# Attention and gated MLP on one core: stores off ScalarE, reciprocals on GpSimd's queue, diagonal copies on ScalarE

## The chip, the cores and the metric

The kernel runs on 1 core of one Trainium2 chip. The metric is device time in microseconds (us) of one execution. A core has five engines with instruction queues of their own: PE (TensorE, matmuls), ACT (ScalarE), DVE (VectorE), POOL (GpSimd) and SP (SyncE, which only issues transfers). Each works through its queue in order; an instruction whose inputs are not there holds up everything behind it. Transfers are issued from SP, ACT or POOL and carried out by 16 DMA engines.

## What is computed

Causal attention in blocks of 64 (8 batches, 8 heads, 576 rows, head size 64), then a gated MLP on its output. In short:

```python
scores = scale * q @ k.T                      # masked by blocks of 64
attn = exp(scores - max) / (sum + 1e-9)
x = (attn @ v)  -> [4608, 512]
gate = 1 / (1 + exp(-(x @ w_gate)))           # w_gate, w_val: 512 x 1536
out = (gate * (x @ w_val)) @ w_out            # w_out: 1536 x 512
```

Precision is kept by splitting each float32 operand into a high and a low part and by three matmuls for each product.

## The kernel before

**Stages.** A *pair* is two heads of one batch; there are 32 pairs (`pairs`), four for each batch. Pairs 0 to 7 follow an order written out by hand (`FRONT`); while that runs, `scripted` is not empty. Pairs 8 to 31 run in the loop at lines 1208 to 1249, and beside their attention the matmuls of the first MLP (the first 512 of the 1536 hidden columns, `mlp1`, `mlp_out`) are dealt out between PE's steps, 36 for each pair. From about 610 us the second MLP (lines 1429 to 1465) does the other 1024 columns and adds the partial results.

**One pair p in the loop**, in the order of `REST`: scores and exponentials (`s`, `t`); then AV of the pair before (`av`, 22 float32 matmuls, which the trace counts as 44; here called AV(p-1)) and its scaling by the reciprocals (`xT`, line 675); block transposes of the exponentials on DVE (`turn`, line 589); preparation of the next pair's keys and queries (`prep`: pm, kl and qx are POOL's part, lines 395, 398 and 408); `move`; `finish` of pair p-1; `recip` of pair p; loads of the keys and queries of pair p+3 (8 transfers) and of the values of pair p+2 (3).

**move (line 591)** is there for pairs 8 to 30 (`moved`). The exponentials lie in `Z` (for odd pairs in the memory of `XB`, which is how the profile then names it) and are rearranged into `G` by 12 transfers of 32 partitions by 800 float32 each, 6 issued on SP and 6 on POOL, and by four copies of the diagonal blocks, 2 on ACT (line 603) and 2 on POOL (line 600). `G` is one buffer: moves of pair p can only start when AV(p-1) has read it, and AV(p) needs them landed.

**recip (line 554).** DVE forms reciprocals of the row sums and transposes them into `rT` (128 x 32). Four transfers on SP store rows 0 to 8 of each of its four 32-row blocks into a DRAM tile `r_d`; three transfers on SP read that back, broadcast over 64 partitions each, into `rb`. `issue` (line 291) keeps transfers on SP behind the last of SP's moves.

**finish (line 799)** of pair p-1: ACT rounds `xT` into `XH` (kept behind the last diagonal copy on ACT), ACT issues the store of `xT` to `xT_d` (288 KB), POOL forms the low part `XL` (kept behind the last of POOL's moves). `out_store` (line 912): ACT halves an MLP result into `ost` and issues its store to `part_d` (256 KB); some one for each pair.

**Order.** Beyond such fixed orders (`behind`) the order of each engine's queue comes from a planner at compile time, which simulates the program and takes what it believes to be ready. On the chip that order is fixed.

Of the kernel before, what the change touches and what calls it, by code (L numbers as in the profile page):

```python
# [9 lines left out]
F32 = mybir.dt.float32  # L10
# [63 lines left out]
def attn_glu_kernel(ctx: ExitStack, tc: tile.TileContext, q, k, v, w_gate, w_val, w_out, out):  # L74
    nc = tc.nc
    B, H, S, D = q.shape
    NTOK, DM = out.shape
    DF = w_gate.shape[1]
    P = 128
# [6 lines left out]
    dram = ctx.enter_context(tc.tile_pool(name="dram", bufs=1, space=DRAM))  # L86
    xT_d = dram.tile([B, DM, S], F32, name="xT_d")
    part_d = dram.tile([NTOK, DM], F32, name="part_d")
# [12 lines left out]
    def behind(ins, other):  # L101

        tc.add_manual_dep(ins, other.name, mybir.DependencyInfo(mybir.DependencyClass.NoSync,
                                                                mybir.DependencyReason.DATA), reason="order")

    def engine_of(queue):

        return "SP" if queue is nc.sync else "ACT" if queue is nc.scalar else "POOL"
# [119 lines left out]
    with ExitStack() as s2:  # L228
# [14 lines left out]
        def x_tiles(b):  # L243

            i = b % 2
            if i not in X:
                X[i] = [(xp0 if i else xp1).tile([P, NC, S], F32R, name=f"X{e}{i}") for e in "HL"]
            return X[i]
# [20 lines left out]
        pairs = [(b, hp) for b in range(B) for hp in range(NP)]  # L269
# [21 lines left out]
        def issue(queue, **kw):  # L291
            ins = queue.dma_start(**kw)  # L292
            if queue is nc.sync and "moves" in last:
                behind(ins.ins, last["moves"])
            return pin(engine_of(queue), ins, True)

        def load(p, what, queue=nc.sync, part=None):
# [33 lines left out]
        last = {}  # L331
        maxima, exps = [], []

        scripted = {}

        def mark(engine, ins):
            last[engine] = ins.ins

        def pin(engine, ins, dma=False):

            if scripted.get("on"):
                for turn in (engine, "DMA") if dma else (engine,):
                    if turn in scripted:
                        behind(ins.ins, scripted[turn])
                    scripted[turn] = ins.ins
                mark(engine, ins)
            return ins
# [24 lines left out]
        def rows(h):  # L372
            return slice(64 * h, 64 * h + 64)
# [47 lines left out]
        def attend(p):  # L421
            b, hp = pairs[p]
            KQ, QB, VS = state.pop(p)
            sm = SMs[p % 2]
            keep = {}
# [12 lines left out]
            Zc = Zs[p % 2].rearrange("p (c x) -> p c x", c=4)  # L438
            Gc = Gt[:, :4 * WB].rearrange("p (a x) -> p a x", a=4)

            def xT_():
                return tile_of("xT", [S])
# [4 lines left out]
            def rb_():  # L447
                return tile_of("rb", [S])
# [3 lines left out]
            moved = N_FIRST < p < len(pairs) - 1  # L452
# [43 lines left out]
            def s_blocks(*groups):  # L496

                maxima.clear()
                exps.clear()
                tiles = [two_banks() for _ in groups]  # L500
                for k, (ps, group) in enumerate(zip(tiles, groups)):
                    for j, i in enumerate(group):
                        scores(ps, i, 2 * P * j)
                        if rest and dealt and k == j == 0:
                            behind(first_mm[0], dealt[-1])
                if rest:
                    hold[:] = pe_last
                for ps, group in zip(tiles, groups):
                    n = P * (group[0] + 1)
                    if len(group) == 1:  # L510
                        nc.vector.memset(ps[0:64, :, n - 64:n], -1e9)
                    else:
                        nc.vector.memset(ps[0:64, :, P:3 * P].rearrange("p h (i n) -> p h i n", i=2)[:, :, :, 64:], -1e9)
                    for j, i in enumerate(group):
                        softmax(ps, i, 2 * P * j)
# [38 lines left out]
            def recip(part=None, queue=nc.sync):  # L554


                if part in (None, 0):
                    pin("DVE", nc.vector.tensor_scalar_add(sm[:, :9], sm[:, :9], 1e-9))
                    pin("DVE", nc.vector.reciprocal(sm[:, :9], sm[:, :9]))
                    keep["rT"] = at.tile([P, 32], F32, name="rT", bufs=2)  # L560
                    mark("DVE", pin("DVE", nc.vector.transpose(out=keep["rT"], in_=sm)))
                if part in (None, 1):
                    keep["r_d"] = dram.tile([9, P], F32, name="r_d", bufs=2)
                    for j in range(4):
                        issue(queue, out=keep["r_d"][:, 32 * j:32 * j + 32], in_=keep["rT"][32 * j:32 * j + 9])
                if part in (None, 2):
                    r_f = keep["r_d"].rearrange("c q -> (c q)")
                    for h, o, n, f in ((0, 0, S, 0), (1, 4 * P, D, S), (1, 0, 4 * P, S + D)):
                        issue(queue, out=rb_()[rows(h), o:o + n], in_=r_f[f:f + n].partition_broadcast(D))

# [15 lines left out]
            def turn(lo, hi):  # L586

                z = Zc[:, :, 32 * lo:32 * hi]
                mark("DVE", nc.vector.transpose(out=z, in_=z))  # L589

            def move():

                turn(LT, NB)
                for k, (c, a) in enumerate(itertools.permutations(range(4), 2)):
                    ins = (nc.sync if k % 2 else nc.gpsimd).dma_start(out=Gc[32 * c:32 * c + 32, a], in_=Zc[32 * a:32 * a + 32, c])  # L595
                    mark("moves" if k % 2 else "POOL", ins)
                for c in range(4):
                    q = slice(32 * c, 32 * c + 32)
                    if c % 2:
                        ins = nc.gpsimd.tensor_copy(out=Gc[q, c], in_=Zc[q, c])  # L600
                        behind(ins.ins, last["POOL"])
                    else:
                        mark("ACT", nc.scalar.copy(out=Gc[q, c], in_=Zc[q, c]))

            def tr_main(i):
                if moved:
# [192 lines left out]
            def finish():  # L799
                XH, XL = x_tiles(b)  # L800
                cut = nc.scalar.copy(out=XH[:, hp], in_=xT_())
                if p == len(pairs) - 1:
                    mark("ACT", cut)
                nc.scalar.dma_start(
                    out=xT_d[b, hp * P:(hp + 1) * P, :], in_=xT_())
                low = nc.gpsimd.tensor_sub(out=XL[:, hp], in0=xT_(), in1=XH[:, hp].bitcast(F32))
                if "POOL" in last and p < len(pairs) - 2:
                    behind(low.ins, last["POOL"])
                    behind(cut.ins, last["ACT"])

            def step(what, is_fine=False, alt=False, queue=nc.sync):
                if is_fine:
                    fine(what, alt, queue)
                elif what == "s":
                    s_blocks((3,), (2,), (1, 0))
                elif what[0] == "s":
                    s_blocks({"s3": (3,), "s2": (2,), "sl": (1, 0)}[what])
                elif what == "t":
                    s_tail()
                elif what == "r":  # L820
                    recip()
                elif what == "trm":
                    if moved:
                        move()
                elif what in ("tr3", "tr2"):
                    tr_main(int(what[2]))
                elif what == "trl":
                    tr_low()
                elif what == "trt":
                    tr_tail()  # L830
                elif what == "fin":
                    finish()
                else:
                    av()
# [77 lines left out]
        def out_store(b, t, po):  # L912
            ost = mp.tile([P, DM], F32, name="t" if b == B and t > 1 else "ost", bufs=2)
            pin("ACT", nc.scalar.mul(out=ost, in_=po, mul=0.5))  # L914

            def store():
                if b < B:
                    r = b * S + t * P
                    pin("ACT", nc.scalar.dma_start(out=part_d[r:r + P, :], in_=ost), True)
                else:  # L920
                    for j in range(2):
                        r = (2 * t + j) * S + NM
                        nc.gpsimd.dma_start(out=part_d[r:r + 64, :], in_=ost[64 * j:64 * j + 64, :])

            return store
# [229 lines left out]
        for item in FRONT.split():  # L1155
            what, where = item.split(".")
            alt = where[-1] == "@"
            queue = nc.scalar if alt else nc.gpsimd if where[-1] == "#" else nc.sync
# [7 lines left out]
            p = int(where)  # L1166
# [41 lines left out]
        for p in range(N_FIRST + 1, n + 1):  # L1208
# [4 lines left out]
            for what, places in REST:  # L1213
# [17 lines left out]
                for _ in range(places if now else 6 if what == "AV" else 0):  # L1231
                    pe_ticks.append(pe_last[0])
                    acc += rate
                    while acc >= 1:
                        acc -= 1
                        left -= 1
                        ins = next(mlp, None)
# [257 lines left out]
```

## Time and profile before

| | us |
|---|---|
| median of 3 runs | 1166.02 |
| the runs | 1158.78 to 1166.15 |
| the profiled execution | 1164.24 |
| its span, first to last instruction | 1162.4 |
| outside the span | 1.8 |
| busy in the span: PE, DVE, ACT, POOL | 1106.7, 850.7, 582.0, 478.8 |

The stretch in which pairs 8 to 30 are worked on runs from about 127 to 505 us. A view of stretches gives the busy time of each engine in it, the granted TensorE clock as a share of 2.4 GHz (0.50 would be the lower level, 1.2 GHz) and the share of time that the 16 DMA engines were busy. In a timeline a row is a start, a duration and the work; `x6` joins six instructions; in brackets stands how long the engine sat idle before it, and what it is believed to have waited for. SPq and ACTq are transfers being issued; their duration is the time that the issuing queue spent.

### The profile page before, as it was taken

What the parts mean: (1) busy time and instruction counts of PE and PEld (TensorE: products, weight loads), DVE (VectorE), ACT (ScalarE), POOL (GpSimd) and SP (SyncE); (2) the same over time, 40 slices, a digit from 0 to 9 for tenths busy, and PEclk for the clock granted to TensorE, in tenths of its full rate; (3) what the DMA queues carried; (4) which work ended last, traced back from release to release, by engine and by line L of the source; (5) the groups of instructions that cost most, each with busy time, mean ns of one, the idle gap of its engine ahead of it and who ended that gap; (6) DMA issues with size and microseconds to landing.
All of it is one profiled execution on the core that took longest, in us unless ns stands there. A gap on an engine that the chain in (4) does not pass through costs nothing.

```text
span 1162.4 us, 19555 instructions
## 1 busy us (share of the span) xinstructions
PE 1106.7 (95%) x6593; PEld 946.8 (81%) x6593; DVE 850.7 (73%) x1482; ACT 582.0 (50%) x1298; POOL 478.8 (41%) x606
## 2 busy tenths in 40 slices
PE   8999989989989998879999999999999999999998
PEld 6677667777767776657889999899999998998998
DVE  7999886777757777738859977876876756756754
ACT  6887665656646665633335444444453332422421
POOL 3655475675656577522002303123033253262350
PEclk9999999999989999979999999999999999999999
DMA  8787577877787788753403335415298445263451
GB/s 171 171 182 167 128 173 187 205 158 192 174 191 158 190 185 164 182 153 107 152 30 109 101 113 208 136 73 208 81 334 281 158 139 171 69 196 116 120 164 55
DMA packets 270692, 181.64 MB, mean 156 GB/s; under 512 B 204576, under 2 KB 225312, under 8 KB 269952
## 3 DMA queue, kind: packets, MB, share of 16 engines
q1 hardware_dynamic: 248080, 143.90, 46.5%
q10 hardware_dynamic: 17712, 21.30, 5.7%
q0 software_dynamic: 4800, 15.19, 5.2%
q8 instruction: 52, 0.85, 0.3%
q14 instruction: 48, 0.39, 0.1%
HBM read 104.73 MB, written 47.33 MB: 131 GB/s over the span
## 4 chain that ended last, share of the span: by engine, by line
PE 70%; DMA 12%; DVE 6%; SPq 5%; issue 3%; ACT 2%; POOL 2%; ACTq 0%; DVEq 0%; POOLq 0%
PE b L1268 30%; PE m L1338 11%; PE bank L351 8%; PE m L179 6%; PE b L1338 6%; PE m L188 4%; SPq L292 3%; DMA G<-XB 3%; PE bank L179 3%; DMA G<-Z 2%; DMA r_d<-rT 1%; DMA XB<-xT_d 1%; DVE Z L589 1%; SPq L595 1%; PE bank L188 1%
## 5 line engine op out<-in xcount | busy, mean ns | idle before, releaser
L1268 PE MATMUL b<-XH,w 128*128 128x384 f32 x1344 | 349.1, 335 | 0.3 <-ACT t L914 0.3
L1268 PEld LDWEIGHTS b<-XH,w 128*128 128x128 f32 x1344 | 243.8, 188 | 4.3 <-ACT t L914 0.7
L1268 PE MATMUL b<-XL,w 128*128 128x384 f32 x672 | 223.5, 335 | 0.0
L351 PE MATMUL bank<-G,VS 128*64 128x64 f32 (+3 forms) x1264 | 110.0, 335 | 27.7 <-DMA r_d<-rT 17.5
L1268 PEld LDWEIGHTS b<-XL,w 128*128 128x128 f32 x672 | 126.1, 188 | 1.7
L351 PEld LDWEIGHTS bank<-G,VS 128*64 128x64 f32 x1264 | 77.8, 154 | 59.6 <-issue 23.8
L1084 POOL TENSOR_TENSOR XB<-XB 128x384 f32<-128x384 f32 x20 | 22.4, 1119 | 238.9 <-DMA XB<-xT_d 169.9
L1338 PE MATMUL m<-wo,hH 128*128 128x512 f32 x368 | 119.9, 391 | 0.0
L188 PE MATMUL m<-wo,hH 128*128 128x512 f32 x256 | 90.0, 403 | 2.7 <-ACT ost L914 2.7
L179 PE MATMUL m<-XH,wg 128*128 128x512 f32 x240 | 86.8, 409 | 0.0
L480 DVE TENSOR_REDUCE nm<-bank 128x2 f32<-128x1024 f32 (+1 forms) x96 | 77.1, 803 | 11.7 <-ACT Z L492 6.0
L1291 ACT ACTIVATE g<-g 128x384 f32<-128x384 f32 x72 | 37.9, 526 | 93.6 <-DVE g L1304 50.6
L179 PE MATMUL m<-XH,wv 128*128 128x512 f32 x240 | 84.4, 401 | 0.0
L1097 ACT CAST XH<-XB 128x1536 fp32r<-128x1536 f32 (+2 forms) x72 | 65.2, 941 | 37.0 <-DVE XB L1095 28.2
L1338 PEld LDWEIGHTS m<-wo,hH 128*128 128x128 f32 x368 | 69.0, 188 | 12.9
L1098 DVE TENSOR_TENSOR XL<-XB,XH 128x1536 fp32r<-128x1536 f32 (+2 forms) x72 | 75.8, 1085 | 0.0
L492 ACT ACTIVATE Z<-bank,nm 128x512 f32<-128x512 f32 (+3 forms) x104 | 53.7, 534 | 37.2 <-DMA G<-XB 16.2
L1338 PE MATMUL m<-wo,hL 128*128 128x512 f32 x184 | 72.1, 392 | 0.0
L1338 PE MATMUL b<-wo,hH 128*128 128x512 f32 (+1 forms) x216 | 71.4, 383 | 0.0
L492 ACT ACTIVATE XB<-bank,nm 128x512 f32<-128x512 f32 (+3 forms) x88 | 45.5, 530 | 37.1 <-DMA G<-Z 19.0
L188 PEld LDWEIGHTS m<-wo,hH 128*128 128x128 f32 x256 | 48.2, 189 | 15.6 <-ACT ost L914 3.5
L1332 POOL TENSOR_TENSOR pr<-pr,pr 128x512 f32<-128x512 f32 x33 | 42.9, 1307 | 41.2 <-DMA pr<-part_d 33.0
(217 smaller groups left out, 2537.5 us busy)
## 6 DMA issues: line engine op xcount, KB each, us to landing
pr<-part_d SPq DMA_DIRECT2D x66, 256.0 KB
xT_d<-xT ACTq DMA_DIRECT2D x32, 288.0 KB
XB<-xT_d SPq DMA_DIRECT2D x16, 576.0 KB
part_d<-pr SPq DMA_DIRECT2D x36, 256.0 KB
rqk<-in_q_dram SPq DMA_DIRECT2D x120, 72.0 KB
rqk<-in_k_dram SPq DMA_DIRECT2D x120, 72.0 KB
out_dram<-pr SPq DMA_DIRECT2D x33, 256.0 KB
part_d<-ost ACTq DMA_DIRECT2D x32, 256.0 KB
```

What stands on the lines that cost most here:

```text
L179: mm = nc.tensor.matmul(ps, lhsT=lh, rhs=rh, start=(i == 0), stop=(i == n - 1))
L188: mm = nc.tensor.matmul(ps, lhsT=lh[:, f, t * P:(t + 1) * P], rhs=rh, start=(f == i == 0), stop=(f == F1 - 1 and i == 2))
L292: ins = queue.dma_start(**kw)
L351: pe_last[:] = [pin("PE", nc.tensor.matmul(*args, **kw)).ins]
L480: mark("DVE", nc.vector.tensor_reduce(out=nm_()[:, c0:c0 + 2], in_=ps[:, :, c:c + n], axis=AX.X, op=ALU.max, negate=True))
L492: mark("ACT", nc.scalar.activation(out=dst, in_=src, func=AF.Exp, bias=nm_()[:, c0 + h:c0 + h + 1], accum_out=sm[:, 5 * h + i:5 * h + i + 1]))
L1097: nc.scalar.copy(out=XO[j][0][:, a:b], in_=x)
L1098: sub = nc.vector.tensor_sub(out=XO[j][1][:, a:b], in0=x, in1=XO[j][0][:, a:b].bitcast(F32))
L1268: mm = nc.tensor.matmul(ps, lhsT=lh, rhs=rh, start=(first and k == 0), stop=(k == n - 1), skip_group_check=not first)
L1291: mark2("ACT", nc.scalar.activation(out=t, in_=c, func=AF.Tanh, scale=0.5))
L1332: nc.gpsimd.tensor_add(out=pr[t], in0=pr[t], in1=other)
L1338: mm = nc.tensor.matmul(po[t][:, cols], lhsT=lh[:, f, t * P:(t + 1) * P], rhs=wo[:, f, e, cols], start=((whole or half == 0) and i == 0), ...
```

## The change

Six edits, all in effect for pairs 8 to 30 and the MLP beside them:

1. `recip` of a moved pair issues on POOL instead of SP. One transfer stores all of `rT` (128 partitions by 128 bytes, `r_d` now 32 rows) instead of four that store 9 rows each.
2. `issue` keeps a transfer on POOL behind `last["POOL"]`: the store of `rT` behind POOL's last move of the pair, and the three broadcasts behind the subtraction `XL` of pair p-1 (`last["low"]`).
3. All four diagonal copies are on ACT, none on POOL.
4. The store of `xT` is issued on SP for all pairs that `finish` handles but the last.
5. The store of `ost` is issued on SP, but for the part under `FRONT` and the last batch.
6. ACT therefore issues no transfer beside pairs 8 to 30.

```diff
         def issue(queue, **kw):
             ins = queue.dma_start(**kw)
             if queue is nc.sync and "moves" in last:
                 behind(ins.ins, last["moves"])
+            if queue is nc.gpsimd and "POOL" in last:
+                behind(ins.ins, last["POOL"])
...
-                    keep["r_d"] = dram.tile([9, P], F32, name="r_d", bufs=2)
-                    for j in range(4):
+                    keep["r_d"] = dram.tile([32, P], F32, name="r_d", bufs=2)[:32 if moved else 9]
+                    if moved:
+                        issue(queue, out=keep["r_d"].rearrange("c (j q) -> j c q", q=32), in_=keep["rT"])
+                    for j in range(0 if moved else 4):
...
+                    if moved:
+                        last["POOL"] = last["low"]
...
-                    if c % 2:
-                        ins = nc.gpsimd.tensor_copy(out=Gc[q, c], in_=Zc[q, c])
-                        behind(ins.ins, last["POOL"])
-                    else:
-                        mark("ACT", nc.scalar.copy(out=Gc[q, c], in_=Zc[q, c]))
+                    mark("ACT", nc.scalar.copy(out=Gc[q, c], in_=Zc[q, c]))
...
-                nc.scalar.dma_start(
+                (nc.sync if p < len(pairs) - 1 else nc.scalar).dma_start(
                     out=xT_d[b, hp * P:(hp + 1) * P, :], in_=xT_())
...
+                    last["low"] = low.ins
...
-                    recip()
+                    recip(None, nc.gpsimd if moved else nc.sync)
...
-                    pin("ACT", nc.scalar.dma_start(out=part_d[r:r + P, :], in_=ost), True)
+                    if scripted or b >= B - 1:
+                        pin("ACT", nc.scalar.dma_start(out=part_d[r:r + P, :], in_=ost), True)
+                    else:
+                        nc.sync.dma_start(out=part_d[r:r + P, :], in_=ost)
```

## Rows read from the trace of the kernel before

**Rows 1.** Busy us by stretch; columns: engines, PEclk, DMA share, GB/s.

```profile
146.50:478.80 332.30, 300.44 (x2143) 236.46 (x2143) 242.99 (x420) 203.29 (x521) 211.27 (x320) 0.95 0.80 180
610.00:1163.00 553.00, 549.26 (x2892) 513.54 (x2892) 390.86 (x666) 216.01 (x377) 166.28 (x151) 1.00 0.44 149
```

**Rows 2.** The same view of two single pairs and of 4 us.

```profile
379.10:393.80 14.70, 14.70 (x111) 11.65 (x112) 12.08 (x21) 9.50 (x25) 9.91 (x15) 1.00 0.72 158
393.80:410.10 16.30, 14.89 (x112) 11.54 (x112) 11.44 (x20) 10.27 (x26) 8.78 (x15) 1.00 0.87 212
...
218.00:222.00 4.00, 2.33 (x38) 2.06 (x40) 4.00 (x6) 3.02 (x9) 2.92 (x3) 1.00 0.36 79
```

**Rows 3.** The chain that ended last, 196 to 262 us, shares by line.

```profile
by line: SPq L292 18.8%; DMA G<-XB 14.1%; PE bank L351 13.0%; PE m L179 9.6%; DMA G<-Z 9.6%; SPq L595 9.1%; DMA xT_d<-xT 7.1%; DMA r_d<-rT 7.0%; DMA rqk<-in_q_dram 5.6%; PE m L188 3.4%; issue 3.0%; DVE Z L589 2.8%; DVE XB L589 1.7%; DVE h L
```

**Rows 4.** SP's timeline: first moves, one whole pair, last moves.

```profile
129.14 4.31 SPq L595 DMA_DIRECT2D G<-Z  x6
...
210.79 5.76 SPq L595 DMA_DIRECT2D G<-XB  x6
216.65 1.55 SPq L292 DMA_DIRECT2D r_d<-rT  x4
218.47 0.87 SPq L292 DMA_DIRECT2D rqk<-in_k_dram  x2
219.53 1.76 SPq L292 DMA_DIRECT2D rb<-r_d  x3
221.33 1.13 SPq L292 DMA_DIRECT2D rqk<-in_k_dram  x2
222.50 2.91 SPq L292 DMA_DIRECT2D rqk<-in_q_dram  x4
225.45 1.98 SPq L292 DMA_DIRECT2D VS<-in_v_dram  x3
227.54 5.17 SPq L595 DMA_DIRECT2D G<-Z  x6
...
493.88 8.23 SPq L595 DMA_DIRECT2D G<-Z  x6
```

**Rows 5.** All engines' timeline, 218 to 236 us: AV, POOL, scaling, AV.

```profile
219.67 2.97 PE L351 MATMUL bank<-G,VS 128*64 128x256 f32 x44 [2.64 <-DMA r_d<-rT]
...
223.53 3.02 POOL L595 DMA_DIRECT2D G<-Z  x6 [0.20 <-issue]
...
224.09 0.82 DVE L675 TENSOR_TENSOR xT<-bank,rb 128x320 f32<-128x320 f32 x2 [1.02 <-DMA rb<-r_d]
...
228.72 1.42 POOL L806 TENSOR_TENSOR XL<-xT,XH 128x576 fp32r<-128x576 f32 x1
...
235.23 0.98 PE L351 MATMUL bank<-G,VS 128*64 128x256 f32 x10 [1.14 <-DMA r_d<-rT]
```

**Rows 6.** ACT's timeline round one store of `ost`.

```profile
327.31 0.60 ACT L914 ACTIVATE ost<-m 128x512 f32<-128x512 f32 x1 [3.03 <-PE m L188]
331.77 0.33 ACTq L919 DMA_DIRECT2D part_d<-ost  x1
332.65 0.69 ACT L492 ACTIVATE XB<-bank,nm 128x512 f32<-128x512 f32 x1 [4.75 <-DMA G<-Z]
```

**Rows 7.** Waits, 127 to 505 us: total us, times, longest.

```profile
ACT XB L492 <- DMA G<-Z: 19.0, 6, 4.8
ACT Z L492 <- DMA G<-XB: 16.2, 6, 3.9
```

**Rows 8.** Single lines: ns min/median/max of one; last, us to landing of L595 on POOL.

```profile
L923 POOL DMA_DIRECT2D part_d<-ost x4: 521/523/554, 609.3 to 610.9; - x4
L600 POOL COPY G<-Z x24: 842/848/852, 133.8 to 496.0; 32x800 f32<-32x800 f32 x24
L603 ACT COPY G<-Z x24: 856/859/865, 129.2 to 491.8; 32x800 f32<-32x800 f32 x24
...
DMA to landing us min/median/max: 2.5/4.6/8.5
```

## The prediction

> **What bounds the kernel now.** The first view to read is that of stretches [rows 1]. From 610 us on PE is busy 549.26 of 553.00 us at full clock: nothing that the change touches is there. From 146.50 to 478.80 us, inside the stretch of pairs 8 to 30, PE is busy 300.44 of 332.30 us at a mean granted clock of 0.95, between the levels 1.2 and 2.4 GHz. That is the part to look into.
>
> How long is a pair there? SP's timeline tells [rows 4]: its first batch of moves starts at 129.14 and its 23rd at 493.88 us, so 364.74 / 22 = 16.58 us for each pair. The window of rows 1 holds 20 of them, 16.6 each. PE's own work in a pair, taken at full clock, is about 300.44 x 0.95 / 20 = 14.3 us (an estimate: it takes busy time to stretch as the clock falls). So each pair loses 2.3 us, part of it waiting, part of it a clock that is low after the waiting.
>
> What does PE wait for? The chain of waits [rows 3] has SP's issuing (lines 292 and 595, 18.8 + 9.1%) and the moves (14.1 + 9.6%) ahead of PE's own lines (13.0, 9.6 and 3.4%). SP's timeline [rows 4] shows why. From 210.79 to 227.54 us, one pair, its issues take 5.76 + 1.55 + 0.87 + 1.76 + 1.13 + 2.91 + 1.98 = 15.96 of 16.75 us. SP has no room. The reader should set this beside the view of all engines [rows 5]: AV ends at 219.67 + 2.97 = 222.64 us and frees `G`; POOL's moves for the next pair begin 0.9 us later, at 223.53, SP's only at 227.54, since broadcasts and loads stand ahead of them. They are issued at 232.71, and AV of the next pair starts at 235.23, after PE sat idle for 1.14 us (2.64 us before the AV at 219.67). The release is put down to `r_d`, which is issued right after the moves; AV does not read it, so I read it as the moves.
>
> A second loss sits on ACT [rows 6]. The `ost` of line 914 is done at 327.91; its store is issued at 331.77, and the exponentials behind it begin at 332.65 after 4.75 us of idleness. They are said to wait for a move, which they do not read; what stands between is the store. Such waits of exponentials sum to 19.0 + 16.2 = 35.2 us in 12 cases [rows 7].
>
> **The change part by part.** SP loses the four stores of `r_d` (1.55 us) and the three broadcasts (1.76), and about 0.5 us of gaps beside them, in which it waited for the stored reciprocals: 16.75 - 3.8 = 12.95 us. It gains two stores in each pair. ACT needs 0.33 us to issue one [rows 6] and I take the like for `xT`; the dearest SP issue is 5.76 / 6 = 0.96. So SP needs 12.95 + 0.66 = 13.6, or up to 12.95 + 1.92 = 14.9 us for a pair. I take 13.6: the 0.96 is that of moves, issued when the DMA engines are full. Where it stood still for reciprocals the transfers stood still too: from 218 to 222 us their share is 0.36 [rows 2].
>
> Moves. With SP free when AV ends, the loop over `G` is AV 2.97, moves on SP 5.2 to 5.8 [rows 4], from the last issue to AV 235.23 - 232.71 = 2.5 (3.1 from 216.55 to 219.67), in all 10.7 to 11.9 us. The planner may put the store of `xT` ahead of the moves; `xT` is done at 224.91 [rows 5], 2.3 us after AV, which makes it 13.0 to 14.2 us. Both lie under PE's 14.3, so that edit costs nothing as long as PE has that work; without this cover it costs up to 2.3 us a pair.
>
> POOL is busy 211.27 / 20 = 10.56 us a pair [rows 1]. Two copies go: 2 x 0.85 = 1.7. Four issues come. The nearest row is a store of 64 rows at 0.52 [rows 8]; the store of `rT` has 128 rows, so 0.52 to 1.04. Together 2.1 to 2.6, and POOL stands at 11.0 to 11.5. The new wait: the broadcasts need `r_d` landed, and it is queued behind POOL's six moves. Landing on this queue takes 2.5 to 8.5 us, 4.6 at the median [rows 8]; on SP's queue the broadcasts began 1.3 us after the last store, 218.20 to 219.53 [rows 4]. `XL`, 1.42 us [rows 5], fits in between, so POOL stands still for 0 to 7.1 us, and I take 4.6 - 1.4 = 3.2, the nearer row being its own queue. POOL then needs 14.2 to 14.7. Behind the broadcasts queue the low parts of the MLP and of the next keys, for which PE would wait next, and the next moves.
>
> Is the reciprocal late? Counted from the end of AV: POOL's moves 0.9 to 3.9, store to 4.7, landed 9.3, broadcasts to 10.9, and landed 2.8 later (221.29 to 224.09 on SP [rows 4, 5]) is 13.7; with 4.6 it is 15.5. The next AV ends a pair later, so `xT` waits for 0 to 0.5 us, against 1.02 now [rows 5].
>
> ACT is busy 203.29 / 20 = 10.2 us [rows 1] and gains 2 x 0.86 = 1.7 [rows 8], 11.9 us, and loses two issues and the waits of 35.2 / 22 = 1.6 us. The copies stand right behind AV and end 1.7 us later than now; the moves land later still, so this is hidden; if it were not, it costs at most 1.7 us a pair.
>
> DMA engines: the bytes are the same but for 92 more rows of 128 bytes in `r_d`. Their share is 0.80 [rows 1]. A rule speaks against such moving about: the Trainium skill, DMA: Bandwidth & Descriptors, Rules for kernel authors, says that spreading transfers over SP, ACT and GpSimd does not help bandwidth, as all run on the same 16 engines, and saves only issue time. By that rule the sum below shrinks to what issue time was worth, and rival B is its extreme; the trace agrees that bytes matter (share 0.80), but shows SP's issuing itself at 15.96 of 16.75 us.
>
> **Sum.** The four needs are PE 14.3, SP 13.6, POOL 14.2 to 14.7, DMA 0.80 x 16.6 = 13.3 at a share of 1. None has much room, so I do not take the floor. The shortest pair of before took 14.7 us, PE without a gap [rows 2]. The densest pair has a DMA share of 0.87 [rows 2], and at that share the same transfers take 13.3 / 0.87 = 15.3. I take their mean, 15.0: 1.58 us less in each of 22 periods, 35 us. From the profiled execution (span 1162.4 and 1.8 outside, 1164.2) that gives 1129.4. The median of the three runs lies 1.8 above it, so 1131.
>
> **The rivals.** (A) *POOL becomes the bound, slower.* If `r_d` lands after 8.5 us instead of 4.6, POOL stands still 7.1 and needs 11.3 + 7.1 = 18.4 us: 1.8 more for 22 pairs, 40 us, 1206. It decides once 11.3 + landing - 1.42 is over 16.6, at a landing of 6.7 us. For it: in-order POOL, its own six moves ahead in the queue, the small margin above. Against: `r_d` has 16 KB where a move has 100, and other POOL work can be planned into the wait.
> (B) *The DMA engines were the bound all along.* Then SP's long issues were the DMA engines' pushing back, and a pair stays 16.6: 1166. For it: moves at 0.96 each on SP against 3.02 / 6 = 0.50 on POOL [rows 4, 5]. Against: 0.87 in one pair, 0.36 in a hole that SP's waiting made [rows 2].
> (C) *The stores hold up SP.* If the store of `ost` stands ahead of the moves and waits for MLP matmuls, as it did 331.77 - 327.91 = 3.9 us on ACT [rows 6], the loop over `G` grows from 11.9 to 15.8, and with the `xT` store ahead too (2.3) to 18.1. With a quarter of the pairs at 18.1 and the rest at 15.8 the mean is 16.4: 0.2 x 22 = 4 us gained, 1162. Against: only some one such store comes in a pair, and the planner can set it behind the moves.
> (D) *The planner changes nothing that matters*, since the order on PE stays and waits shift: as B.
>
> **How the numbers follow.** Forecast 0.65, A 0.14, B with D 0.12, C 0.09. The forecast's own bounds: PE's floor 14.3 in all periods, 50 us gained, 1116; and 15.7 us a pair (SP's dearest issues and 0.8 of gaps), 19 us, 1147. A measurement of this kernel tells about 1% from no change. Faster by over 1% (below 1154) takes the forecast and a third of C, where fewer pairs meet it: 0.68. Within 1%: B, D, the rest of C, and a mild A: 0.19. Slower: the rest of A, 0.13. The range leaves out A beyond no change and a little below the floor: 1114 to 1167.
>
> **What would show it.** Right: between batches of SP's moves about 15 us, these starting within 3 us of AV's end; the exponentials' waits for moves gone; clock near 1 between 146 and 460 us. A would show as POOL idle for over 5 us until `r_d` lands, and PE or DVE waiting for KL, hL or `rb`; B as SP issues still long with a DMA share still near 0.80 to 0.87 and the pair at 16.6; C as SP idle ahead of line 595 until ACT or DVE is done. The prediction is wrong if the stretch after 610 us changes, as nothing here says it should.

## The result and the profile after

The changed kernel takes 1116.56 us (median of 4 runs, 1114.15 to 1117.68), against 1165.29 for the kernel before: a ratio of 0.9591, interval 0.9552 to 0.9629, so 48.7 us or 4.1% faster. Forecast were 1131 us and a range of 1114 to 1167. The profiled execution took 1117.68 us, its span 1115.9: 46.5 us below that of before.

First the view of stretches, as in [rows 1]: 20 pairs, then the second MLP.

```profile
143.68:441.50 297.82, 286.95 (x2142) 227.95 (x2143) 253.67 (x421) 237.21 (x560) 221.24 (x360) 0.99 0.94 199
563.50:1116.00 552.50, 549.23 (x2893) 513.44 (x2892) 387.58 (x666) 216.65 (x378) 167.08 (x152) 1.00 0.44 149
```

A pair takes 297.82 / 20 = 14.9 us where it took 16.6, PE is busy in 96% of the stretch at a clock of 0.99 instead of 90% at 0.95, and its work at full clock is 286.95 x 0.99 / 20 = 14.2 us, as before. The second MLP is unchanged: 549.2 us of PE in both. Now SP's timeline, to be set beside [rows 4]: first moves, one pair, last moves.

```profile
128.54 3.76 SPq L601 DMA_DIRECT2D G<-Z  x6
...
246.25 3.72 SPq L601 DMA_DIRECT2D G<-Z  x6
250.40 0.35 SPq L925 DMA_DIRECT2D part_d<-ost  x1
250.85 0.40 SPq L806 DMA_DIRECT2D xT_d<-xT  x1
251.30 4.25 SPq L292 DMA_DIRECT2D rqk<-in_k_dram  x4
255.60 2.17 SPq L292 DMA_DIRECT2D rqk<-in_q_dram  x4
257.81 1.75 SPq L292 DMA_DIRECT2D VS<-in_v_dram  x3
259.66 1.01 SPq L925 DMA_DIRECT2D part_d<-ost  x2
260.78 3.73 SPq L601 DMA_DIRECT2D G<-XB  x6
...
455.05 3.70 SPq L601 DMA_DIRECT2D G<-Z  x6
```

The seven reciprocal transfers are gone, the stores have come. In this pair, with three stores of `ost`, SP issues for 3.72 + 0.35 + 0.40 + 4.25 + 2.17 + 1.75 + 1.01 = 13.65 of 14.53 us. From the first to the 23rd batch of moves it is (455.05 - 128.54) / 22 = 14.84 us a pair, against 16.58. That is 22 x 1.74 = 38.3 us. The mean over these 22 pairs is 13.48 us of issuing against 15.63 before, and SP's moves now start 0.0 to 2.9 us after AV ends, where they started 1.3 to 6.7 us after it. Another 7.6 us lie behind the last batch of moves: 1162.4 - 493.88 = 668.5 us before, 1115.9 - 455.05 = 660.9 after; the first batch comes 0.6 earlier. Together 46.5.

Waits beside pairs 8 to 30 (127 to 460 us; total, times, longest), those rows that the forecast is about. POOL also waits 36.8 us for ACT's `hH` and 25.3 us for `KQ`:

```profile
POOL rb L292 <- DMA r_d<-rT: 22.3, 10, 3.6
DVE xT L677 <- DMA rb<-r_d: 19.6, 9, 4.9
PE bank L353 <- DMA rqk<-in_k_dram: 5.9, 6, 2.1
PE bank L353 <- DVE xT L677: 5.3, 3, 2.2
ACT XB L494 <- DMA G<-Z: 3.3, 3, 1.4
ACT ost L917 <- DMA part_d<-ost: 1.6, 4, 1.0
ACT Z L494 <- DMA G<-XB: 0.8, 1, 0.8
```

The exponentials' 35.2 us of waits put down to moves [rows 7] have become 4.1. POOL does stand still for `r_d`, but for 22.3 us in 23 pairs. What POOL issues (line 292, ns min/median/max; the last row is the landing in us of the store and the broadcasts together):

```profile
L292 POOL DMA_DIRECT2D rb<-r_d x66: 516/526/592, 139.5 to 451.8; - x66
L292 POOL DMA_DIRECT2D r_d<-rT x23: 729/734/738, 133.6 to 459.9; - x23
...
DMA to landing us min/median/max: 2.4/4.3/9.3
```

### The profile page after: what moved, and what is told of

It reads as the page before. It is cut to its first block, busy times and chain, and to the rows that moved or that the text cites. A ratio compares the mean times of both kernels' runs of the same rounds, so it can differ in the third digit from the quotient of the medians.

```text
span 1115.9 us, 19504 instructions
## 1 busy us (share of the span) xinstructions
PE 1089.3 (98%) x6593; PEld 935.9 (84%) x6593; DVE 858.8 (77%) x1482; ACT 621.7 (56%) x1344; POOL 490.3 (44%) x652
## 4 chain that ended last, share of the span: by engine, by line
PE 74%; DMA 7%; SPq 6%; DVE 5%; POOL 3%; issue 3%; ACT 2%; ACTq 0%; DVEq 0%; POOLq 0%
PE b L1274 31%; PE m L1344 11%; PE m L179 8%; PE bank L353 7%; PE b L1344 6%; PE m L188 4%; SPq L292 4%; PE bank L179 3%; DMA rqk<-in_k_dram 3%; SPq L601 1%; DMA rb<-r_d 1%; DMA rqk<-in_q_dram 1%; PE bank L188 1%; DVE KQ L385 1%; DMA VS<-in_v_dram 1%
## 5 line engine op out<-in xcount | busy, mean ns | idle before, releaser
L353 PE MATMUL bank<-G,VS 128*64 128x64 f32 (+3 forms) x1264 | 96.9, 308 | 8.7 <-DMA rqk<-in_k_dram 5.9
L353 PEld LDWEIGHTS bank<-G,VS 128*64 128x64 f32 x1264 | 68.1, 139 | 35.9 <-issue 4.8
L494 ACT ACTIVATE Z<-bank,nm 128x512 f32<-128x512 f32 (+3 forms) x104 | 53.6, 532 | 16.6 <-DVE nm L482 8.6
L218 POOL TENSOR_TENSOR hL<-h,hH 128x512 fp32r<-128x512 f32 x27 | 35.3, 1307 | 45.8 <-ACT hH L214 45.5
```

The lines of the kernel that those rows point to most:

```text
L353: pe_last[:] = [pin("PE", nc.tensor.matmul(*args, **kw)).ins]
L494: mark("ACT", nc.scalar.activation(out=dst, in_=src, func=AF.Exp, bias=nm_()[:, c0 + h:c0 + h + 1], accum_out=sm[:, 5 * h + i:5 * h + i + 1]))
```

## The experiments

Two theories stood at the start. *Theory 1*: SP's issuing was the bound and the move of the reciprocals (edits 1 and 2) gives the gain. *Theory 2*: ACT, held up in front of its own stores, was the bound, and edits 4 to 6 give it. A third came with the results, on the order that the planner makes on POOL. Each edit is shown against the changed kernel; `...` stands for lines left out.

All ratios are to the kernel before, run beside (its medians there were 1161.8 to 1165.3 us). "Pair" is the time between SP's first and last batch of moves over 22; "rest" is from the start of the last batch to the end of the span.

| kernel | median us | ratio, interval | pair us | rest us |
|---|---|---|---|---|
| before | 1165.3 | | 16.58 | 668.5 |
| changed | 1116.6 | 0.9591 (0.9552 to 0.9629) | 14.84 | 660.9 |
| no_recip | 1163.5 | 1.0014 (0.9998 to 1.0031) | 16.66 | 663.9 |
| refill | 1147.6 | 0.9874 (0.9853 to 0.9896) | 16.00 | 667.0 |
| one_store_sp | 1140.1 | 0.9786 (0.9770 to 0.9803) | 15.76 | 667.5 |
| no_stores | 1128.6 | 0.9699 (0.9673 to 0.9725) | 15.50 | 660.2 |
| no_copies | 1190.8 | 1.0232 (1.0187 to 1.0277) | 17.70 | 661.9 |
| copies_ordered | 1181.6 | 1.0147 (1.0110 to 1.0185) | 17.78 | 662.3 |
| recip_ordered | 1203.8 | 1.0339 (1.0300 to 1.0379) | 18.45 | 665.5 |
| after_ordered | 1122.1 | 0.9632 (0.9615 to 0.9649) | 15.06 | 658.3 |
| copies_kl | 1120.7 | 0.9621 (0.9596 to 0.9646) | 14.92 | 662.2 |
| recip_kl | 1137.5 | 0.9774 (0.9747 to 0.9802) | 15.70 | 660.6 |
| store_sp | 1111.2 | 0.9549 (0.9516 to 0.9582) | 14.42 | 660.8 |
| store_sp_again | 1111.5 | 0.9562 (0.9528 to 0.9595) | 14.50 | 661.0 |

### SP's issuing: no_recip, refill, one_store_sp

**no_recip** undoes edits 1 and 2.

```diff
...
-                    keep["r_d"] = dram.tile([32, P], F32, name="r_d", bufs=2)[:32 if moved else 9]
-                    if moved:
-                        issue(queue, out=keep["r_d"].rearrange("c (j q) -> j c q", q=32), in_=keep["rT"])
-                    for j in range(0 if moved else 4):
+                    keep["r_d"] = dram.tile([32, P], F32, name="r_d", bufs=2)[:9]
+                    for j in range(4):
...
-                    recip(None, nc.gpsimd if moved else nc.sync)
+                    recip()
```

> The change without its first two edits: reciprocals stay on SP with four stores and three broadcasts, while the two kinds of stores are on SP and all diagonal copies on ACT. Theory 1 (SP's issuing was the bound): SP needs its old 16.0 us and two issues more, 0.7 to 1.9, so 16.7 to 17.9 us a pair: no gain or slower, 1165 to 1190 us. Theory 2 (ACT's stalls at its stores were the bound): most of the gain stays, 1117 to 1135 us.

1163.5 us: the other four edits alone bring nothing. Just below the range of theory 1, far from theory 2. Here is where ACT's waits went (127 to 505 us):

```profile
ACT ost L913 <- DMA part_d<-ost: 39.0, 10, 6.4
```

ACT no longer stands in front of its stores, but `ost` has two buffers, and the store that must have read one is now late on SP's queue, which issues for 15.1 of 16.7 us a pair and waits for the stored reciprocals besides. The stall has moved by one step.

**refill** gives SP its seven issues back, without bytes or waits.

```diff
+                if moved:
+                    spare = dram.tile([7, 9, 32], F32, name="spare", bufs=2)
+                    for j in range(7):
+                        issue(nc.sync, out=spare[j], in_=keep["rT"][32 * (j % 4):32 * (j % 4) + 9])
```

> The changed kernel with seven small stores of rT (9 rows of 128 bytes each) issued on SP behind the moves of each moved pair, to a DRAM tile that nobody reads: SP gets back the number of issues that the change took from it, with no wait and hardly a byte. Theory 1: SP needs 13.3 + 7 x 0.3 to 0.4 = 15.4 to 16.1 us a pair against 14.8 now: 13 to 28 us more, 1129 to 1145 us. Theory 2, and the rival that the DMA engines' bytes bound SP: no change, 1115 to 1120 us.

1147.6 us, 31 more than the changed kernel and 3 above the range of theory 1: 22 x 1.16 = 25.5 in the pairs and 6.1 behind the last moves. One pair of it on SP:

```profile
303.74 3.73 SPq L605 DMA_DIRECT2D G<-XB  x6
307.57 0.53 SPq L810 DMA_DIRECT2D xT_d<-xT  x1
308.15 3.41 SPq L292 DMA_DIRECT2D spare<-rT  x7
311.65 2.85 SPq L292 DMA_DIRECT2D rqk<-in_k_dram  x4
314.54 2.39 SPq L292 DMA_DIRECT2D rqk<-in_q_dram  x4
316.98 2.76 SPq L292 DMA_DIRECT2D VS<-in_v_dram  x3
319.84 4.04 SPq L605 DMA_DIRECT2D G<-Z  x6
```

Seven issues that move some 8 KB take 3.41 us, SP is full again, and most of the time goes back. This is the most direct evidence: it is the issuing on SP that sets the time, not the bytes. It does not go back one to one: over 22 pairs the seven issues take 2.97 us each time, SP's issuing grows by 1.49 (13.48 to 14.97) and the pair by 1.16, since the key loads behind them take 2.3 us instead of 3.5. The wait of ACT for `ost` is back too, 34.6 us in 10 cases. Behind the last moves, the exponentials of pair 31 wait 6.4 us for them, which they do not in the changed kernel.

**one_store_sp** leaves the reciprocals on SP, with one store instead of four.

```diff
-                    if moved:
-                        last["POOL"] = last["low"]
...
-                    recip(None, nc.gpsimd if moved else nc.sync)
+                    recip()
```

`recip` without a queue issues on SP; the one store of the changed kernel stays.

> As no_recip (reciprocals on SP), with one store of rT instead of four: three issues fewer on SP in each pair, the round trip through DRAM unchanged. Theory 1: SP's need falls by 3 x 0.4 = 1.2 us a pair from the 16.0 that no_recip's batches of moves show: 22 to 26 us less than no_recip, 1137 to 1145 us. If the wait for the round trip was what held SP: no change, 1160 to 1165 us.

1140.1 us, inside the range of theory 1. Three issues fewer make 23 us against no_recip, half of the whole gain, with the round trip through DRAM still on SP. The stores of `rT` take 0.60 us of SP a pair instead of 1.57, and the pair is 0.90 us shorter.

### The stores: no_stores

```diff
-                (nc.sync if p < len(pairs) - 1 else nc.scalar).dma_start(
+                nc.scalar.dma_start(
...
-                    if scripted or b >= B - 1:
-                        pin("ACT", nc.scalar.dma_start(out=part_d[r:r + P, :], in_=ost), True)
-                    else:
-                        nc.sync.dma_start(out=part_d[r:r + P, :], in_=ost)
+                    pin("ACT", nc.scalar.dma_start(out=part_d[r:r + P, :], in_=ost), True)
```

> The change without edits 4 to 6: the stores of xT and ost stay on ACT; reciprocals are on POOL and all copies on ACT. Theory 1: SP needs 13.0 us a pair, PE binds, 1116 to 1125 us; the exponentials' waits behind ACT's stores shrink with SP's backlog. Theory 2: the stalls of ACT remain (1.6 us a pair or more), 1140 to 1160 us.

1128.6 us, between the two theories: 12 us lost. So edits 4 to 6 are worth something, but only with SP freed. ACT waits in front of exponentials 7.2 us in 3 cases for `xT_d`, which the changed kernel does not.

### The copies: no_copies, copies_ordered, copies_kl

**no_copies** undoes edit 3.

```diff
-                    mark("ACT", nc.scalar.copy(out=Gc[q, c], in_=Zc[q, c]))
+                    if c % 2:
+                        ins = nc.gpsimd.tensor_copy(out=Gc[q, c], in_=Zc[q, c])
+                        behind(ins.ins, last["POOL"])
+                    else:
+                        mark("ACT", nc.scalar.copy(out=Gc[q, c], in_=Zc[q, c]))
```

> The change without edit 3: two diagonal copies stay on POOL. Theory 1 and 2 alike: POOL has 1.7 us more a pair. If POOL stands still for r_d for about 1 us a pair, as the trace of after shows (22.3 us in 10 cases), it has room for them: 1115 to 1120 us. If POOL is near its bound (theory 3, POOL is next): broadcasts and next moves come 1.7 us later, up to 1150 us.

1190.8 us: slower than the kernel before, 41 us past the worst that was expected. POOL's timeline of one pair, from its moves to the next:

```profile
303.15 2.96 POOL L601 DMA_DIRECT2D G<-Z  x6
306.15 1.75 POOL L606 COPY G<-Z 32x800 f32<-32x800 f32 x2
307.85 0.73 POOL L292 DMA_DIRECT2D r_d<-rT  x1
309.86 1.42 POOL L812 TENSOR_TENSOR XL<-xT,XH 128x576 fp32r<-128x576 f32 x1 [1.27 <-ACT XH L807]
313.19 1.28 POOL L218 TENSOR_TENSOR hL<-h,hH 128x512 fp32r<-128x512 f32 x1 [1.90 <-ACT hH L214]
315.66 0.52 POOL L397 TENSOR_SCALAR KQ<-KQ 128x128 f32<-128x128 f32 x1 [1.18 <-DVE KQ L385]
316.17 1.42 POOL L400 TENSOR_TENSOR KL<-KQ,KH 128x576 fp32r<-128x576 f32 x1
317.54 0.81 POOL L410 CAST QBH<-QH 64x64 fp32r<-64x64 f32 x2
318.41 0.52 POOL L410 CAST QBL<-QL 64x64 fp32r<-64x64 f32 x2
318.88 1.63 POOL L292 DMA_DIRECT2D rb<-r_d  x3
320.49 2.96 POOL L601 DMA_DIRECT2D G<-XB  x6
```

The broadcasts (`rb`) stand at the very end, 11 us after the store, behind the work on the next keys and queries, though nothing holds them up when their turn comes. In the changed kernel they stand ahead of that work in all pairs but two; here the planner set them behind it in 22 of 23. So theory O: it is their place in the order and not the 1.7 us of the two copies (theory P).

**copies_ordered** was to test this and kept only line 397 behind the broadcasts.

```diff
-                    pin("POOL", nc.gpsimd.tensor_scalar_mul(KQ[:, 1, :P], KQ[:, 1, :P], scale))
+                    ins = pin("POOL", nc.gpsimd.tensor_scalar_mul(KQ[:, 1, :P], KQ[:, 1, :P], scale))
+                    if "rb" in last:
+                        behind(ins.ins, last["rb"])
...
```

> As no_copies (two diagonal copies on POOL), with one more fixed order: POOL's first instruction for the next pair's queries (line 397) stays behind the broadcasts. In no_copies the planner set that instruction and the low parts of keys and queries ahead of the broadcasts in 22 of 23 pairs, in the changed kernel it did not. Theory O (the place of the broadcasts in POOL's order did it): 1117 to 1130 us. Theory P (POOL's 1.7 us a pair did it): still 1175 to 1195 us.

1181.6 us, by which theory O would have fallen. POOL's timeline of it says why it does not:

```profile
298.71 1.42 POOL L402 TENSOR_TENSOR KL<-KQ,KH 128x576 fp32r<-128x576 f32 x1 [0.49 <-ACT KH L390]
...
301.02 1.57 POOL L292 DMA_DIRECT2D rb<-r_d  x3
302.67 0.52 POOL L397 TENSOR_SCALAR KQ<-KQ 128x128 f32<-128x128 f32 x1
```

The low part of the keys (line 402 there) does not depend on line 397, and still stood ahead of the broadcasts. The experiment had not done what it was meant to do. **recip_ordered**, edits 1 and 2 alone under the same order, shared the fault:

> Edits 1 and 2 alone (reciprocals on POOL with one store; stores stay on ACT, two copies on POOL), with the same fixed order. Theory 1 (SP's issuing was the bound) with O: nearly all of the gain, less the 12 us that the stores were worth in no_stores: 1125 to 1140 us. If edits 3 to 6 are needed for it: 1150 us or more.

1203.8 us, with SP issuing for only 13.6 us of each pair: a pair takes 18.45 us, and PE waits 56.7 us in 19 cases for `xT`. Moving the reciprocals without the other edits, in this order, made the kernel 3.4% slower.

**copies_kl** is no_copies with all of the work on the next keys and queries kept behind the broadcasts.

```diff
...
-                        pin("POOL", nc.gpsimd.tensor_sub(out=KS[1], in0=KQ[:, 0], in1=KS[0].bitcast(F32)))
+                        ins = pin("POOL", nc.gpsimd.tensor_sub(out=KS[1], in0=KQ[:, 0], in1=KS[0].bitcast(F32)))
+                        if "rb0" in last:
+                            behind(ins.ins, last["rb0"])
...
```

The same two lines stand behind the casts of the queries.

> As no_copies (two diagonal copies on POOL), with the broadcasts of pair p fixed ahead of all of POOL's work on the keys and queries of pair p+2 (lines 397, 400, 410 of no_copies). copies_ordered fixed only line 397, and its broadcasts still stood behind the low part of the keys, just ahead of the next moves. Theory O (the broadcasts' place in POOL's order): 1117 to 1135 us. Theory P (POOL's 1.7 us a pair): 1175 to 1195 us as no_copies.

1120.7 us, 70 us less than no_copies, with the very same instructions. So theory P falls: POOL has the same work in both, and the order makes the difference. POOL in copies_kl:

```profile
300.29 1.42 POOL L822 TENSOR_TENSOR XL<-xT,XH 128x576 fp32r<-128x576 f32 x1
...
303.59 1.58 POOL L292 DMA_DIRECT2D rb<-r_d  x3
305.19 0.56 POOL L397 TENSOR_SCALAR KQ<-KQ 128x128 f32<-128x128 f32 x1
```

PE's waits in no_copies, then the same line in copies_kl (127 to 460 us each):

```profile
PE bank L353 <- DVE xT L681: 24.3, 9, 4.9
PE bank L353 <- ACT XB L494: 15.9, 6, 2.7
```

```profile
PE bank L353 <- DVE xT L691: 1.5, 3, 1.0
```

Late broadcasts make `xT` late, `xT` reads PSUM, and PE's next scores wait for that bank. At the median over the pairs the last broadcast is issued 3.6 us after AV ends in no_copies and 0.2 us after it in copies_kl, and `xT` starts 7.8 and 3.8 us after AV ends. Little of this shows as a wait of `xT` for `rb` (17.5 and 20.3 us in all), because the planner changed DVE's order too: in 19 of 23 pairs of no_copies `xT` stands behind maxima of the next scores, in copies_kl never. That order alone is not the loss: store_sp below, the fastest kernel, has it in 19 of 23 pairs as well. With the order fixed, two copies on POOL cost 1120.7 against 1116.6, with intervals that overlap. Edit 3's own work is worth some 4 us, not clear of the noise; its effect was that the planner set the broadcasts early.

**recip_kl** is edits 1 and 2 alone with that order.

> Edits 1 and 2 alone with the same fixed order as copies_kl: reciprocals on POOL with one store, stores on ACT, two copies on POOL. Theory O with theory 1: 12 us more than copies_kl, 1129 to 1147 us, against 1203.8 for recip_ordered. Theory P: about 1200 us.

1137.5 us. In steps: reciprocals on POOL with the right order 27 us, stores off ACT 17 (1137.5 to 1120.7), copies on ACT some 4, within the noise.

**after_ordered** fixes line 397 in the changed kernel.

```diff
...
+                    if "rb" in last:
+                        behind(ins.ins, last["rb"])
...
```

> The changed kernel with the same fixed order, which its planner kept on its own in all but two pairs. Theory O: the same or a few us better, 1110 to 1118 us.

1122.1 us, 4 above the range and with an interval that overlaps the changed kernel's. It did not help; why it may be worse was not pursued.

### A version that goes further: store_sp

```diff
-                        issue(queue, out=keep["r_d"].rearrange("c (j q) -> j c q", q=32), in_=keep["rT"])
+                        issue(nc.sync, out=keep["r_d"].rearrange("c (j q) -> j c q", q=32), in_=keep["rT"])
```

> The changed kernel with the one store of rT issued on SP behind SP's moves, the broadcasts still on POOL. POOL's wait for r_d (22.3 us in 10 cases in the changed kernel) should shrink, since the store no longer queues behind POOL's moves; SP gets one issue of 0.4 us, for which it has room. If the reciprocals' round trip still costs the changed kernel time: 1108 to 1114 us. If PE alone binds: 1115 to 1118 us.

1111.2 us, in the range of the first case, but not for the reason given:

```profile
POOL rb L292 <- DMA r_d<-rT: 70.0, 21, 5.5
DVE xT L677 <- DMA rb<-r_d: 9.6, 10, 3.8
```

POOL's wait for `r_d` did not shrink, it grew from 22.3 to 70.0 us. The wait of `xT` halved, from 19.6 to 9.6. POOL's timeline shows the broadcasts right behind `XL` in 18 of 23 pairs, with only an `hL` in between in the other five, so they are issued as soon as `r_d` is there; POOL has the time to wait. Whether the earlier store or this earlier place of the broadcasts gave the gain was not separated. The pair is at 14.42 us, PE busy in 98% of the stretch (284.87 of 289.50) at a clock of 1.00, and PE's floor of 14.2 is nearly reached. The same kernel once more:

> The kernel of store_sp once more, unchanged, in more rounds, since its interval against before (0.9516 to 0.9582) and that of the changed kernel (0.9552 to 0.9629) overlap. If it is truly the faster one: 1108 to 1113 us and a ratio under 0.957 with its whole interval below the changed kernel's 0.9591. If the 5 us were chance: about 1116 us.

1111.5 us, 5 us below the changed kernel a second time (3 by the ratios), but the interval (up to 0.9595) just includes 0.9591. Likely faster by 3 to 5 us; not proven by these runs.

## Why the prediction was right, and where it was off

**What bounds.** Right. SP's issuing set the time: refill shows it by issues put back, one_store_sp by issues taken away, and no_recip, which leaves them all on SP, gains nothing.

**SP's need.** Right in the sum, in part by luck. Taken were 13.6 us; 13.48 is the mean of the 22 pairs. But the forecast kept the prices of one pair of before, and they moved in opposite directions: six moves took 5.17 to 5.76 us there and 3.72 in the pair shown above, four key loads 0.87 + 1.13 = 2.0 there and 4.25 here, and the two stores 1.12 us on average instead of 0.66. An issue has no fixed price: no_stores, without the stores on SP, issues for 13.55 us a pair as well. What I had not seen is that a full SP also takes from ACT what the stores gave it, by the buffers of `ost`: this is rival C's stall, on ACT instead of SP, in no_recip and refill. C itself did not come: SP's 21 stores of `ost` waited for ACT for 3.2 us in all.

**POOL.** Its busy time is 221.24 / 20 = 11.1 us (11.0 to 11.5 forecast), a broadcast 0.53 (0.52), the store 0.73 (0.52 to 1.04). The stall for `r_d` was mis-sized: 3.2 us a pair forecast, 22.3 / 23 = 1.0 measured. Landing is as slow as I took it, 4.3 us for store and broadcasts together, but the low parts of the MLP and casts lie in between too. The prediction's wait of `xT` for `rb`, 0 to 0.5, is 19.6 / 23 = 0.85, and before it was 11.2 / 23 = 0.5: here the change made things worse, and store_sp gets part of it back.

**The copies.** The step that was wrong in kind. I costed edit 3 as 1.7 us of POOL against a hidden 1.7 us on ACT, and rival A as a late landing. The loss that lay there was another: the planner's order. Without edit 3 the change is slower than before by 2.3%, without edits 3 to 6, under much the same order, by 3.4%. The sum took for granted that the broadcasts would stand ahead of the next keys and queries. The forecast had no way of telling which order would come; that this one came was luck, and its chance of 0.14 for a slower kernel through POOL was about a real danger with a wrong mechanism: POOL's longest wait for `r_d` in the changed kernel is 3.6 us.

**DMA engines.** I let 0.87 of share, the densest pair, pull the pair up to 15.3. The trace of after has 0.94 over 20 pairs, 0.94 x 14.9 = 14.0 us where it was 13.3, and store_sp 0.97. A share near 1 was no wall at these levels, and the trace of before had already shown that the reading passes 1:

```profile
242.00:246.00 4.00, 4.00 (x32) 3.12 (x31) 2.39 (x4) 1.51 (x4) 3.69 (x6) 1.00 1.22 222
```

So rival B falls: the pair is shorter with nearly the same bytes. That 15.0 came so near to 14.84 owes something to this wrong term, which was averaged with a floor of 14.7.

On the rule of the Trainium skill (DMA: Bandwidth & Descriptors, Rules for kernel authors) that spreading transfers over queues saves only issue time: the trace agrees, and here issue time was what was short. The page adds (Issuing engines are not separate DMA queues) that this time is usually small beside the transfer. In refill SP spent 3.41 us on issuing some 8 KB; how long those transfers took themselves the trace does not show.

**The sum.** A pair of 15.0 us was forecast, 14.84 measured: 35 us against 38.3. The rest of the difference, 7.6 us, is a term that was left out: the stretch behind the last batch of moves. There SP was late in the kernel before as well. The exponentials of pair 31 in before, then PE's waits from 478 to 610 us before, and from 440 to 560 us after:

```profile
504.01 0.69 ACT L492 ACTIVATE Z<-bank,nm 128x512 f32<-128x512 f32 x1 [8.89 <-DMA G<-Z]
```

```profile
PE bank L351 <- ACT Z L492: 5.5, 1, 5.5
PE bank L356 <- ACT Z L551: 3.2, 1, 3.2
```

```profile
PE bank L353 <- DVE xT L677: 2.7, 1, 2.7
```

SP took 8.23 us for the last moves of before [rows 4] and 3.70 after; the exponentials of pair 31 overwrite what these read, and waited 8.9 us for them. The other kernels with a full SP show this wait too, 5.4 us in no_recip, 6.4 in refill and 7.8 in one_store_sp; in the rest it is at most 1.9. So it goes with a full SP, the same cause in a place where I had not counted it. How much of the 7.6 us it makes is not shown: no_recip has the wait and a rest of 663.9 us.

## What to carry to other kernels

Count a queue's issues and set their sum against the period before looking at bytes: a queue at 95% of its time with small transfers was a bound here like any engine. Merging issues came before moving them in value here: one store instead of four, with edits 3 to 6, gave half of the gain. When waiting instructions are moved to an engine whose order a planner makes, read the order that comes out: the same instructions cost 1120.7 or 1190.8 us here, and half of the change, taken alone, was slower than none. A stall that is taken from one engine's queue can come back through the buffers that the moved transfer holds.

## What the runs showed of the hardware

Issues on SP in the kernel before, ns min/median/max, of 9 rows of 128 bytes and of 72 KB:

```profile
L292 SPq DMA_DIRECT2D r_d<-rT x92: 264/313/1968, 133.6 to 504.8; - x92
L292 SPq DMA_DIRECT2D rqk<-in_k_dram x84: 333/498/1563, 137.3 to 471.3; - x84
```

So 1.1 KB cost 0.31 us at the median (0.49 with the gap to the next in refill's row, 3.41 / 7), and 64 times as much only 0.50. The longest were 3 to 6 times the median; what makes an issue long was not taken apart. On POOL the price went with the rows, not with the bytes: 0.50 us for 32 rows and 100 KB, 0.53 for 64 rows of a broadcast, 0.73 for 128 rows and 16 KB. The DMA engines' busy share rose to 0.97 over 20 pairs without PE losing more than 2% of the stretch, and the share times the pair's length rose from 13.3 to 14.0 us with nearly the same bytes (180 x 16.6 and 199 x 14.9 give 3.0 MB each), so a share is no fixed amount of work.
